# Moving a few dense matmuls around the second attention logits, units 18 to 31

## The chip, the cores and the metric

The kernel runs on one core of one Trainium2 chip. The metric is device time in microseconds (us). TensorE does the matmuls, ScalarE the exponentials and copies, VectorE the elementwise work, GpSimd the masks, and SyncE's queue (SP) the transfers.

## The reference

The input is x, 2048 tokens by 1024. It is layer-normalised to xn, and the output is x + A(xn) + B(xn). B is a token-mixing MLP; it is done before the part at issue. A is attention in four segments of 512 tokens, 32 heads of 32, with a memory carried from segment to segment:

```
q, k, v = x @ wq, x @ wk, x @ wv        # split into heads and 4 segments
for s in range(4):
    p = softmax(qs @ ks.T * scale + causal_mask)
    a_dot = p @ vs
    a_mem = (phi(qs) @ M) / (phi(qs) @ z + 1e-6)   # phi(t) = t+1 if t>0 else exp(t)
    o = g * a_mem + (1 - g) * a_dot
    M, z = M + phi(ks).T @ vs, z + sum(phi(ks))
return o @ wo
```

Matrices are bf16, sums are in float32.

## The kernel before

The first 375 us or so do the norm and the MLP and leave its sum in the output buffer. Then `attention` runs 32 units: unit u is segment u // 8 and a group of four heads, u % 8. An even unit is followed by an odd one, and some of the work is shared by the pair.

The order of the work on every engine is written out by hand. In one unit TensorE does:

- **Logits** of unit u (`logits`, line 1349), in steps. Step 0 holds the first block of keys, step 1 the second and fourth, step 2 (even units only) the third block of this unit and of the next one. Each step fills the four PSUM banks 0 to 3 and is followed by one exponential of 128x2048 on ScalarE (line 1370), which frees these banks, and by masks on GpSimd (line 1374), one per key block. The text calls the steps first, second and third logits.
- **Weighing** of unit u-1 (`weigh`, line 1379), in three parts W0, W1, W2: probabilities times values, and phi(q) times the memory. W0 and W2 use bank 4, W1 bank 5. After each part VectorE copies the result out (ost, line 1424), so W2 waits for the copy of W0. Up to weighing of unit 23, W2 also has four matmuls with pk that update the memory.
- **Dense** matmuls (`dense`, line 1326), which fill the time that the logits and the weighing would wait for other engines. They come from a queue of jobs of eight matmuls of 128x512: value projections (wv), query projections (wq) and output projections of an earlier segment (wo). Jobs alternate between banks 6 and 7. At its eighth matmul a job issues its copy out: ScalarE for wv (vA, line 1299) and wq (qT, line 1253), VectorE for wo (fin, line 1313). A wq job also issues the load of the weights of two units later, on SP.

How many dense matmuls stand in each place is set by `cut`: the unit's total is divided by a tuple of shares, rounded cumulatively. For an even unit the places are: before first logits, before W0, before W1, before W2, before second logits, before third logits, and the rest. An odd unit has no third logits, so its places end with "the rest" after second logits. From unit 18 an even unit has 24 dense matmuls, an odd one 20 and unit 31 has 16.

VectorE's chain for unit u-1 (scales, phi of q, `products`, line 1473, and `add`, line 1479), and then the transpose of its result by SP (oT), are put out one step at a time at stops within the dense jobs (`side`). In even units from 18 on, `products` is done in two halves. `late_exps` puts ScalarE's exponential for phi behind a logits exponential. After unit 31, `tail` does the last output projections.

For units below 18, and for odd units from 18, the shares before the change are:

```
elif u < 10 or u >= 14 and total <= 26:
    cuts = self.cut(total, (0, 4, 2, 4, 1, 13, 8) if even else (7, 3, 2, 4, 1, 15))
```

Of the kernel before, what the change touches and what calls it, by code (L numbers as in the profile page):

```python
# [386 lines left out]
class _Kernel:  # L387
# [1143 lines left out]
    def attention(self):  # L1531
        self.jobs, self.turn, self.left = deque(), 0, 0
        self.side, self.stops = deque(), self.STOPS
        self.exps, self.in_etmp = [], [None] * 4
        self.wo_jobs = deque((c, half) for c in range(4 * (N_SEG - 1)) for half in range(2))
        self.jobs.extend([self.q_job(0), self.k_job(0)] + [self.v_job(0, c) for c in range(4)])
        self.dense(16)
        self.late_exps()
        self.phi_k(0)
        self.k_transpose(0)  # L1540
        self.jobs.extend([self.q_job(1), self.k_job(1)])
        self.dense(100)
        for u in range(N_UNIT):
            if u == N_GRP:
                t, R = _Walk(self.mem, self.B_AT + self.STG_AT, self.B_AT + self.S2_AT).take(
                    "oT2", [P, N_GRP, SEG_L], BF16, N_GRP)
                self.oT.append(t)
                self.R_oT.append(R)
                self.load_fin(0)
                self.load_fin(1)  # L1550
            if 1 <= u <= N_GRP:
                self.fw.dma(self.wo[:, u - 1, :], self.A_wo[(u - 1) * P:u * P, :], writes=[self.R_wo[u - 1]])
            even = u % 2 == 0
            self.jobs.extend(self.unit_jobs(u))
            total = 8 * len(self.jobs) - sum(j[0] for j in self.jobs) - self.left
            xn = self.XN_AT.index(u) + 4 if u in self.XN_AT else None
            if u in self.XN_AT[::4]:
                self.xn_load(xn)
                self.xn_load(xn + 1)
            if u >= 18 and even:  # L1560
                cuts = self.cut(total, (0, 5, 1, 4, 0, 9, 5))
            elif u < 10 or u >= 14 and total <= 26:
                cuts = self.cut(total, (0, 4, 2, 4, 1, 13, 8) if even else (7, 3, 2, 4, 1, 15))
            else:
                cuts = self.cut(total, (0, 4, 2, 2, 2, 14, 8) if even else (7, 3, 2, 2, 2, 16))
            end = u >= N_UNIT - 4
            self.stops = self.STOPS_FEW if total <= 26 and u >= 14 else self.STOPS
            self.dense(cuts[0])
            self.logits(u, 0)
            self.dense(cuts[1], end)  # L1570
            while end and self.side:
                self.side.popleft()()
            if u:
                self.weigh(u - 1, 0)
            self.dense(cuts[2], False)
            if u:
                self.weigh(u - 1, 1)
            self.dense(cuts[3], False)
            if u:
                self.weigh(u - 1, 2)  # L1580
                steps = self.combine(u - 1)
                last = steps[-1]
                steps[-1] = lambda u=u, last=last: (last(), self.o_transpose_dma(u - 1))
                self.side.append(steps.pop(0))
            if N_GRP <= u:
                self.side.append(lambda u=u: self.phi_q(u))
            if u:
                self.side.extend(steps)
            if u + 1 < N_UNIT:
                self.side.append(lambda u=u: (self.phi_k(u + 1), self.k_transpose(u + 1)))  # L1590
            if xn is not None:
                self.side.append(lambda c=xn: (self.xn_scale(c), self.xn_transpose(c), c % 4 < 2 and self.xn_load(c + 2)))
            self.dense(cuts[4])
            self.logits(u, 1)
            if even:
                self.dense(cuts[5])
                self.logits(u, 2)
            self.dense(8 * len(self.jobs) - sum(j[0] for j in self.jobs) - self.left)
        while self.side:
            self.side.popleft()()  # L1600
        self.tail()
# [84 lines left out]
```

## Time and profile before

| | us |
|---|---|
| median of 4 runs | 651.4 (651.3 to 651.52) |
| the profiled execution | 651.63 |
| its span | 649.9 |
| TensorE busy | 639.6 |
| VectorE busy | 435.0 |
| ScalarE busy | 282.3 |
| GpSimd busy | 152.2 |
| one exponential of 128x2048 (line 1370, mean of 80) | 1.877 |
| one mask (line 1374, median of 128) | 0.635 |

Times within a profile count from the start of its span. Units 18 to 31 begin at 530.96. The first logits of the even units 18, 20, ... 30 start at 530.96, 545.67, 560.68, 575.54, 590.27, 604.59 and 618.85. The granted TensorE clock is full in all slices. Matmuls are pipelined, so a row's end reaches into the next row: what counts is the distance from start to start. A row "x5" merges five instructions. A few matmul records are missing; a row then shows one matmul less than the order has, with an unexplained gap of about one matmul beside it.

### The profile page before, as it was taken

Reading aid. Unit: us, or ns where it says so; the run is one execution under the profiler, and the core shown is the slowest. Engines: PE = TensorE matmul, PEld = TensorE weight load, DVE = VectorE, ACT = ScalarE, POOL = GpSimd, SP = SyncE. Lnnn points to the kernel's source line nnn. Section 1 sums busy time; section 2 is a strip of 40 time slices with the busy share of each in tenths; the row PEclk is TensorE's granted clock in tenths of the full one; section 3 lists DMA queues with packets and bytes.
Section 4 is the critical chain, followed back from the end, with each engine's and each line's share of the span. In section 5 each row is a group of like instructions: output and inputs, shape, how many; then the busy total and the mean of one; then the engine's idle time right before and its main releaser. Section 6 shows DMA issues by size and latency. Waiting matters only on the chain.

```text
span 649.9 us, 11137 instructions
## 1 busy us (share of the span) xinstructions
PE 639.6 (98%) x4559; PEld 303.6 (47%) x4611; DVE 435.0 (67%) x813; ACT 282.3 (43%) x307; POOL 152.2 (23%) x179
## 2 busy tenths in 40 slices
PE   8999999999999999999999999999999999999998
PEld 3444444444444444444444444444455454445544
DVE  6975676665556664744637326766887888787896
ACT  7543222232210000110101037778777878889770
POOL 2500000000001220220202203343334444454440
PEclk9999999999999999999999999999999999999999
DMA  8804233233498937538272957989863666445334
GB/s 300 219 0 131 66 104 91 65 113 83 122 261 199 244 113 210 147 112 227 72 219 84 265 126 184 185 177 209 140 143 93 161 163 126 122 104 129 102 96 139
DMA packets 190123, 95.00 MB, mean 146 GB/s; under 512 B 108664, under 2 KB 176248, under 8 KB 190072
## 3 DMA queue, kind: packets, MB, share of 16 engines
q1 hardware_dynamic: 189928, 94.25, 57.3%
q8 instruction: 36, 0.59, 0.4%
q14 instruction: 15, 0.12, 0.1%
q10 hardware_dynamic: 144, 0.03, 0.0%
HBM read 69.23 MB, written 11.53 MB: 124 GB/s over the span
## 4 chain that ended last, share of the span: by engine, by line
PE 93%; DVE 2%; ACT 2%; DMA 2%; issue 1%; POOL 0%; DVEq 0%
PE ps_all L199 93%; ACT pT L1370 1%; DMA w2s<-in_B_w_dram 1%; DVE ln_st L587 1%; DVE sum L648 0%; DMA xin<-in_A_x_dram 0%; DVE h L627 0%; POOL ln_rs L611 0%; DVE part L689 0%; ACT qT L1253 0%; ACT vA L1299 0%; DVE gT L663 0%; DVE ln_mv L590 0%; DVE ln_mv L609 0%; DVE fin L1632 0%
## 5 line engine op out<-in xcount | busy, mean ns | idle before, releaser
L1370 ACT ACTIVATE pT<-ps_all 128x2048 bf16<-128x2048 f32 x80 | 150.2, 1877 | 43.4 <-PE ps_all L199 42.8
L1374 POOL TENSOR_SCALAR_AFFINE_SELECT pT<-pT 128x512 bf16<-128x512 bf16 x128 | 103.7, 828 | 161.7 <-ACT pT L1370 161.7
L689 DVE TENSOR_TENSOR part<-ps_all,part 128x512 f32<-128x512 f32 x84 | 57.7, 690 | 108.9 <-PE ps_all L199 87.9
L1075 POOL TENSOR_TENSOR part<-part,stg 128x512 f32<-128x512 f32 x24 | 33.0, 1402 | 285.4 <-DVE part L689 268.5
L746 ACT ACTIVATE g<-part,b1c 128x512 f16<-128x512 f32 x36 | 26.0, 722 | 99.0 <-DVE part L689 99.0
L199 PE MATMUL ps_all<-wv,xnT 128*128 128x512 bf16 x240 | 64.6, 380 | 1.3 <-ACT qT L1253 0.2
L199 PE MATMUL ps_all<-wo,oT 128*128 128x512 bf16 (+2 forms) x258 | 61.0, 366 | 1.4 <-issue 0.5
L199 PE MATMUL ps_all<-xnT,wq 128*128 128x512 bf16 x240 | 61.3, 380 | 0.5 <-issue 0.3
L694 ACT ACTIVATE part<-ps_all 128x512 f32<-128x512 f32 x24 | 14.0, 596 | 101.7 <-PE ps_all L199 67.1
L199 PEld LDWEIGHTS ps_all<-vA,pT 128*128 128x128 bf16 x1280 | 45.9, 96 | 19.3 <-DVE ost L1424 1.2
L1424 DVE TENSOR_TENSOR ost<-ps_all,eps 128x396 bf16<-128x396 f32 (+1 forms) x72 | 36.9, 520 | 26.2 <-PE ps_all L199 25.7
L199 PE MATMUL ps_all<-g,sum 128*128 128x512 f16 x224 | 51.0, 379 | 0.0
L199 PE MATMUL ps_all<-g,w2s 128*128 128x512 f16 x224 | 51.0, 379 | 0.0
L199 PE MATMUL ps_all<-gT,sum 128*128 128x512 f16 x224 | 50.3, 379 | 0.1
L199 PE MATMUL ps_all<-vA,pT 128*128 128x33 bf16 x1280 | 48.5, 177 | 0.0
L199 PE MATMUL ps_all<-h,sum 128*128 128x512 f16 x192 | 45.2, 379 | 0.0
L199 PE MATMUL ps_all<-h,w1s 128*128 128x512 f16 x192 | 44.9, 379 | 0.0
L199 PE MATMUL ps_all<-hT,sum 128*128 128x512 f16 x192 | 43.6, 379 | 0.0
L1473 DVE TENSOR_TENSOR prod<-ost,srec 128x1024 bf16<-128x1024 bf16 (+1 forms) x31 | 35.9, 1158 | 0.3
L199 PEld LDWEIGHTS ps_all<-wo,oT 128*128 128x128 bf16 x272 | 23.9, 97 | 24.4 <-issue 3.7
L199 PEld LDWEIGHTS ps_all<-xnT,wq 128*128 128x128 bf16 x256 | 22.6, 97 | 25.4 <-issue 5.3
L199 PEld LDWEIGHTS ps_all<-gT,sum 128*128 128x128 f16 x224 | 21.8, 98 | 26.8 <-DVE gT L663 0.6
(119 smaller groups left out, 861.8 us busy)
## 6 DMA issues: line engine op xcount, KB each, us to landing
w2s<-in_B_w_dram SPq DMA_DIRECT2D x8, 1792.0 KB, 9.8
w1s<-in_B_w_dram SPq DMA_DIRECT2D x12, 1024.0 KB, 5.6
wq<-in_A_wq_dram SPq DMA_DIRECT2D x32, 256.0 KB, 3.4
xs<-in_A_x_dram SPq DMA_DIRECT2D x24, 256.0 KB, 3.4
stg<-in_A_x_dram SPq DMA_DIRECT2D x16, 256.0 KB, 2.9
out_dram<-stg SPq DMA_DIRECT2D x16, 256.0 KB, 4.3
wk<-in_A_wk_dram SPq DMA_DIRECT2D x16, 256.0 KB, 3.6
fin<-out_dram SPq DMA_DIRECT2D x16, 256.0 KB, 3.3
```

What stands on the lines that cost most here:

```text
L199: ins = self.nc.tensor.matmul(*args, **kwargs)
L587: fw.op("dve", lambda e: e.bn_stats(st[:, 6 * h:6 * h + 6], src[:, 512 * h:512 * h + 512]), reads=[self.R_xin[c]], writes=[R])
L689: self.fw.op("dve", lambda e: e.tensor_tensor(self.tmp[dst][:], self.bank(b), self.tmp[src][:], op=ALU.add), reads=[self.R_bank[b], self.R ...
L694: self.fw.op("act", lambda e: e.activation(self.tmp[dst][:], self.bank(b), ACT.Copy), reads=[self.R_bank[b]], writes=[self.R_tmp[dst]])
L746: self.fw.op("act", lambda e: e.activation(self.gB[f % 2][half][:, f // 2, :], src, ACT.Gelu_apprx_tanh, bias=self.b1c[:, f:f + 1], scale= ...
L1075: fw.op("pool", lambda e: e.tensor_tensor(self.tmp[t][:], self.tmp[t][:], self.stg[k][:, 512 * half:512 * half + 512], op=ALU.add), reads= ...
L1370: fw.op("act", lambda e: e.activation(dst, src, ACT.Exp, scale=SCALE), reads=self.R_bank[0:4], writes=[R[v % 2][kb] for v, kb, _ in blocks ...
L1374: fw.op("pool", lambda e: e.affine_select(d, d, pattern=[[0, 4], [1, P]], compare_op=ALU.is_ge, fill=0.0, base=0, channel_multiplier=-1), ...
L1424: fw.op("dve", lambda e: e.tensor_tensor(dst, src, eps, op=ALU.add), reads=[self.R_bank[b], self.R_eps], writes=[self.R_ost[o][part]])
L1473: fw.op("dve", lambda e: e.tensor_tensor(self.prod[:, a0:a1], ost[:, a0:a1, 0:D_HEAD], rec[:, a0:a1].unsqueeze(2).to_broadcast([P, a1 - a0 ...
```

## The change

Only shares are changed. Even units from 18 get one share fewer in front of W2 and one more between second and third logits. Odd units from 18 get shares of their own. The jobs, their order and the number of instructions on every engine stay.

```diff
             if u >= 18 and even:
-                cuts = self.cut(total, (0, 5, 1, 4, 0, 9, 5))
+                cuts = self.cut(total, (0, 5, 1, 3, 0, 10, 5))
+            elif u >= 18:
+                cuts = self.cut(total, (4, 1, 2, 1, 0, 12))
             elif u < 10 or u >= 14 and total <= 26:
                 cuts = self.cut(total, (0, 4, 2, 4, 1, 13, 8) if even else (7, 3, 2, 4, 1, 15))
```

## The prediction

> **What bounds the kernel now.** I read the page first: busy rows, the chain that ended last.
>
> ```profile
> PE 639.6 (98%) x4559; PEld 303.6 (47%) x4611; DVE 435.0 (67%) x813; ACT 282.3 (43%) x307; POOL 152.2 (23%) x179
> PE 93%; DVE 2%; ACT 2%; DMA 2%; issue 1%; POOL 0%; DVEq 0%
> ```
>
> TensorE sets the end. A new order of the same matmuls can only win or lose TensorE's idle moments, so I looked for those in units 18 to 31 (530.96 us to the end), first in TensorE's timeline, then in those of its weight loads, ScalarE, VectorE and GpSimd.
>
> ```profile
> 542.66 0.39 PE L199 MATMUL ps_all<-vA,pk 128*128 128x132 bf16 x4
> 543.20 0.40 PE L199 MATMUL ps_all<-qT,kT 32*128 32x384 bf16 x8
> 543.53 1.25 PE L199 MATMUL ps_all<-xnT,wq 128*128 128x512 bf16 x5
> 544.62 1.03 PE L199 MATMUL ps_all<-wo,oT 128*128 128x512 bf16 x4
> 545.67 0.40 PE L199 MATMUL ps_all<-qT,kT 32*128 32x512 bf16 x4
> ```
>
> Unit 19, from the end of its third weighing part (W2) to unit 20's first logits. The prices are here: five dense matmuls from 543.53 to 544.62 are 0.217 us each; a logits group takes 0.33. The four wo matmuls should end at 545.49. A dense-to-logits turn costs 0.10 where nothing is waited for (536.66 plus three matmuls to 537.41), so unit 20's logits should start at 545.58. They start 0.09 later.
>
> ```profile
> 543.65 1.88 ACT L1370 ACTIVATE pT<-ps_all 128x2048 bf16<-128x2048 f32 x1 [1.04 <-PE ps_all L199]
> 545.42 0.59 ACT L1253 ACTIVATE qT<-ps_all 128x512 bf16<-128x512 f32 x1
> 546.11 1.88 ACT L1370 ACTIVATE pT<-ps_all 128x2048 bf16<-128x2048 f32 x1
> ```
>
> ScalarE's exponential of the second logits ends at 545.53; the next logits need the same four banks. Started 0.45 after its logits, it ends 2.33 after them, and nine dense matmuls don't quite cover that.
>
> ```profile
> 545.64 0.13 PEld L199 LDWEIGHTS ps_all<-qT,kT 32*128 32x128 bf16 x4 [0.49 <-issue]
> 549.00 0.47 PEld L199 LDWEIGHTS ps_all<-vA,pT 128*128 128x128 bf16 x16 [0.39 <-DVE ost L1424]
> 561.14 0.77 PEld L199 LDWEIGHTS ps_all<-wv,xnT 128*128 128x128 bf16 x5 [0.36 <-issue]
> ```
>
> Weight loads show three kinds of stop: this one; W2 of unit 20, which waits for VectorE to empty its bank; and unit 22's first dense matmuls, whose bank ScalarE's late vA copy holds until 561.03.
>
> ```profile
> 544.77 0.69 DVE L1230 SCALAR_TENSOR_TENSOR pqT<-qT,mtmp 128x512 bf16<-128x512 bf16 x1
> 545.38 1.72 DVE L1473 TENSOR_TENSOR prod<-ost,srec 128x512 bf16<-128x512 bf16 x2
> 547.80 0.68 DVE L1313 TENSOR_TENSOR fin<-ps_all,fin 128x512 bf16<-128x512 f32 x1
> 548.40 1.03 DVE L1424 TENSOR_TENSOR ost<-ps_all,eps 128x396 bf16<-128x396 f32 x2
> 537.42 1.04 POOL L1374 TENSOR_SCALAR_AFFINE_SELECT pT<-pT 128x512 bf16<-128x512 bf16 x1 [3.29 <-ACT pT L1370]
> 537.88 1.66 DVE L1473 TENSOR_TENSOR prod<-ost,srec 128x1024 bf16<-128x1024 bf16 x1
> 552.20 1.72 POOL L1374 TENSOR_SCALAR_AFFINE_SELECT pT<-pT 128x512 bf16<-128x512 bf16 x1 [3.51 <-ACT pT L1370]
> 552.21 1.22 DVE L1473 TENSOR_TENSOR prod<-ost,srec 128x1024 bf16<-128x1024 bf16 x1
> ```
>
> VectorE runs without a break from unit 19's W2 to unit 20's ost copies. The last four lines are two meetings of VectorE's product with GpSimd's masking: whoever comes second is held.
>
> **The change part by part.** It adds and removes no instruction; it moves dense matmuls within a unit. The cuts (rounded shares) give more than its words say: with 20 matmuls an odd unit goes from 4, 2, 2, 2, 1, 9 to 4, 1, 2, 1, 0, 12. Second logits come three dense matmuls sooner, W2 two, W0 and W1 one. Even units go from 0, 5, 1, 4, 0, 9, 5 to 0, 5, 1, 3, 0, 10, 5: W2 and second logits one sooner, third logits unmoved. Unit 31 (16 matmuls) goes from 4, 1, 1, 2, 0, 8 to 3, 1, 2, 0, 0, 10: its first logits come one sooner, too.
>
> *Gain 1, first logits of units 20, 22, 24, 26, 28, 30.* All start 2.46 or 2.47 after the second logits before them (545.67, 560.68, 575.54, 590.27, 604.59, 618.85), where 2.38 is the work between. Twelve matmuls in place of nine cover ScalarE with 0.56 to spare: 6 x 0.09 = 0.54.
>
> *Gain 2, banks held by a copy behind that exponential.* Unit 22 stands 0.17 (561.01 to 561.18), units 26 and 30 0.07 each. The exponential, 0.65 earlier, lets the copy through in time: 0.31. Two like stops, 0.25 in unit 21 and 0.16 in unit 25, come after an even unit's third logits; their qT copy is behind third logits' exponential, which doesn't move, so they stay.
>
> *Gain 3, W2 of units 20 and 24.* They wait 0.06 each. In even units W2 arrives 0.217 sooner, at 548.64 in unit 20 (with 0.09 from gain 1). Its bank is free 0.61 after the first ost copy starts. VectorE's unbroken chain starts from unit 19's W2, 0.43 sooner: copy at 547.97, bank free at 548.58. The wait goes: 0.12. What covers the even unit's part is thus the odd unit's; without it this edit costs 0.217 a unit. Elsewhere the bank is free in time: in unit 18, where no chain moves, 533.89 against W2's arrival at 534.01.
>
> *Loss, unit 31.* Only eight matmuls are left between unit 30's third logits and unit 31's first: 0.217 of waiting for the exponential. Then 0.33 + 3 x 0.217 + weighing 1.24 + 0.10 = 2.32 lies before second logits, which can't start before 2.38: 0.06. Together 0.27, and all dense work after it is TensorE's own.
>
> *At nothing.* Odd second logits wait for first logits' exponential, 2.38 later at the earliest; the work between is 2.77 (with the four pk matmuls) or 2.54 (from unit 25), so 0.16 to spare. Odd W2 needs its bank 0.79 after W0's end and has 1.07. Masking comes earlier with its exponential. On SP, in units 19, 23 and 27 the q-weight load falls behind the oT transpose: from 544.81 to about 548.7, landing 3.4 later, needed near 558.8; transposes go 0.4 earlier and key loads stay. In unit 31 a fin sum moves behind an ost copy and holds VectorE's chain about 0.5; unit 30's transpose moves from 636.31 to about 636.8, lands 2.4 later and is needed at 639.9. If those covers fail, the tail waits by the excess. Other engines' order is unchanged.
>
> *A rule against the change.* The product 537.88 took 1.66 beside a mask begun first; 552.21, which won, took 1.22: the loss is 0.44. The Trainium skill (SBUF — State Buffer, section "SBUF: two separate sides") says that VectorE's two-input operations and GpSimd share one port pair: "The shared pair is an **exclusive lock**", held for a whole instruction. In unit 19 the product leads the mask by 0.21. The chain moves 0.43, the mask 0.65: a dead heat in units 19, 21, 23. From unit 25 the product led by 0.61 and keeps the lead. By the rule a lost heat costs a whole mask, 0.63 (its usual time); by the row 0.44. Then unit 20's ost copy starts at 548.41, W2 leaves at 549.02 as before, gains 1 and 3 are lost there (0.15), and the matmul moved behind it is added, 0.217: 0.37 each in units 20 and 24, so the sum is +0.04 by the row, +0.42 by the rule. Unit 22 has no fin sum in the way and stands. I take the heat as won: in 552.20 against 552.21 the mask was recorded 0.01 earlier and lost.
>
> Sum: -0.54 - 0.31 - 0.12 + 0.27 = -0.70 us. The profiled execution took 651.63 (span 649.9), 0.23 over the median of 651.4; taken to the median, 650.7.
>
> **Rivals.**
> - *Heat lost*: GpSimd holds VectorE; no net change, 651.4 (651.8 by the rule). For it: the waiting mask won at 537.42. Against: it came 0.46 before the product there.
> - *Less than the sum*: part of the 0.09 is not ScalarE. For it: the trace puts 545.64 down to "issue". Against: unit 18, reached with an older exponential, shows none. Only gains 2, 3 and the loss: 651.2.
> - *More*: unit 21's and 25's stops go with the earlier copies, another 0.41: 650.3.
> - *Slower*: W2 of every even unit stands for its bank, since VectorE does not come forward. All seven moved matmuls are then lost, 7 x 0.217 = 1.52, gains before that point are absorbed, and the 0.27 stays: +1.79, 653.2. It decides where the first ost copy ends later than W2 arrives. Units 28 and 30 would be 0.04 short (606.99 + 0.61 against 607.56) if the chain did not gain its 0.43; units 18, 22 and 26 have 0.12 to 0.3 to spare even then, which speaks against it.
> - *The words aren't the change*: three matmuls instead of two, and unit 31, are counted above; with odd units at two the cover in gain 1 would still be ample.
>
> **How the numbers follow.** My sum 0.47, heat lost 0.23, less 0.12, more 0.10, slower 0.08. The range 650.0 to 652.0 leaves out the slower rival and the edges of the rest. A measurement of this kernel can tell about 0.2%, 1.3 us, from no change: faster means under 650.1, slower over 652.7. All forecasts but "slower" lie inside. Faster 0.10 (most of "more", if it is underrated by 0.2, and a little of my sum), within 0.82, slower 0.08. For the likeliest case alone: 650.3 to 651.0.
>
> **What would show it.** Right: first logits of units 20 to 30 start 0.10 after the last dense matmul; unit 22's dense matmuls follow its logits in 0.33; W2 in units 20 and 24 shows no VectorE wait; a new stop near 0.2 before unit 31's first logits. Wrong: products of 2.1 us in units 19, 21 and 23, weight loads of even W2 waiting for ost, or a wait before jc 6 of the tail's products. A span shorter by over 1.3 or longer at all disproves my sum.

## The result, and the profile after

The changed kernel takes 650.77 us (median of 34 runs), the kernel before 651.51 (52 runs). The ratio is 0.9989, 95% interval 0.9984 to 0.9993: 0.74 us or 0.1% less, and the interval leaves out 1. The profiled execution took 650.8, its span is 649.0.

The busy row of the page after:

```profile
PE 639.5 (99%) x4559; PEld 304.2 (47%) x4611; DVE 435.5 (67%) x813; ACT 282.7 (44%) x307; POOL 153.3 (24%) x179
```

TensorE works as long as before (639.5 against 639.6), in a shorter span. The page cannot say where the idle time went. The starts of the first logits do. Counted from unit 18's first logits of the same trace (530.96 before, 530.83 after: the 0.13 arose in code that the change does not touch), in us; the ends of the spans are taken from the traces to 0.01 (649.89 and 649.03):

| | before | after | difference | summed from the prediction's steps |
|---|---|---|---|---|
| unit 20 | 14.71 | 14.62 | -0.09 | -0.09 |
| unit 22 | 29.72 | 29.47 | -0.25 | -0.24 |
| unit 24 | 44.58 | 44.08 | -0.50 | -0.50 |
| unit 26 | 59.31 | 58.63 | -0.68 | -0.65 |
| unit 28 | 73.63 | 72.79 | -0.84 | -0.81 |
| unit 30 | 87.89 | 86.95 | -0.94 | -0.90 |
| unit 31 | 96.56 | 95.55 | -1.01 | -0.97 |
| end of the span | 118.93 | 118.20 | -0.73 | -0.70 |

TensorE's timeline after, from unit 19's W2 to unit 20's first logits:

```profile
542.10 0.39 PE L199 MATMUL ps_all<-vA,pk 128*128 128x132 bf16 x4
542.42 0.40 PE L199 MATMUL ps_all<-qT,kT 32*128 32x384 bf16 x8
542.98 1.67 PE L199 MATMUL ps_all<-xnT,wq 128*128 128x512 bf16 x7 [0.16 <-issue]
544.49 1.03 PE L199 MATMUL ps_all<-wo,oT 128*128 128x512 bf16 x4
545.45 0.39 PE L199 MATMUL ps_all<-qT,kT 32*128 32x512 bf16 x4
```

Second logits follow W2 at once, and twelve dense matmuls follow them (eight wq, of which one record is missing in front of 542.98, and four wo). The wo matmuls should end at 544.49 + 4 x 0.217 = 545.36, and unit 20's logits start at 545.45: only the turn's 0.09 to 0.10 is left.

ScalarE in the same place:

```profile
542.87 1.88 ACT L1370 ACTIVATE pT<-ps_all 128x2048 bf16<-128x2048 f32 x1 [0.40 <-PE ps_all L199]
545.90 1.88 ACT L1370 ACTIVATE pT<-ps_all 128x2048 bf16<-128x2048 f32 x1 [0.61 <-PE ps_all L199]
```

Second logits' exponential ends at 544.75, 0.70 ahead of the logits that need its banks. Before, these were 0.14 apart; and now it is ScalarE that waits 0.61 for TensorE.

Unit 22's dense matmuls, which had to wait for their bank before, now follow its logits (560.30 + 0.33):

```profile
560.62 0.76 PEld L199 LDWEIGHTS ps_all<-wv,xnT 128*128 128x128 bf16 x5 [0.23 <-issue]
```

Every block begins with some idle time of the weight loads: 0.20 to 0.23 in front of dense matmuls, 0.42 to 0.43 at a turn to logits. The loads of units 18 to 31 that stand longer are these, and unit 24's W2, which reads as unit 20's:

```profile
548.45 0.52 PEld L199 LDWEIGHTS ps_all<-vA,pT 128*128 128x128 bf16 x16 [0.27 <-DVE ost L1424]
554.82 0.10 PEld L199 LDWEIGHTS ps_all<-wv,xnT 128*128 128x128 bf16 x1 [0.45 <-issue]
584.22 0.10 PEld L199 LDWEIGHTS ps_all<-wv,xnT 128*128 128x128 bf16 x1 [0.39 <-ACT qT L1253]
626.37 0.10 PEld L199 LDWEIGHTS ps_all<-qT,kT 32*128 32x128 bf16 x4 [0.64 <-ACT pT L1370]
```

The first is W2 of unit 20: the load is released by VectorE, but the matmul follows when the dense ones end (547.87 + 3 x 0.217 = 548.52, started 548.51), so the 0.27 costs nothing. The next two are the stops of units 21 and 25 behind the qT copy, which stayed. The last is new: unit 31's first logits, with a matmul less in front of them.

VectorE and GpSimd at the place of the dead heat:

```profile
544.82 1.72 DVE L1473 TENSOR_TENSOR prod<-ost,srec 128x512 bf16<-128x512 bf16 x2
546.58 0.74 DVE L1479 TENSOR_TENSOR o_s<-prod 128x512 bf16<-128x512 bf16 x1
547.84 1.03 DVE L1424 TENSOR_TENSOR ost<-ps_all,eps 128x396 bf16<-128x396 f32 x2
544.82 2.22 POOL L1374 TENSOR_SCALAR_AFFINE_SELECT pT<-pT 128x512 bf16<-128x512 bf16 x2 [2.13 <-ACT pT L1370]
```

Product and mask start at the same hundredth, and the product wins: 1.72 as before, and the two masks take 2.22 instead of 2.01. The row of the product is two instructions, one for each half. The first half takes 0.68; the second, while the first mask runs, takes 1.00, before as after. So to win here means that the first half is not held.

In the tail a product of the same kind lost. Unit 30's product and add, and the masks of unit 31, after; then product and add before:

```profile
631.75 2.15 DVE L1473 TENSOR_TENSOR prod<-ost,srec 128x512 bf16<-128x512 bf16 x2
634.43 0.41 DVE L1479 TENSOR_TENSOR o_s<-prod 128x512 bf16<-128x512 bf16 x1
631.15 2.21 POOL L1374 TENSOR_SCALAR_AFFINE_SELECT pT<-pT 128x512 bf16<-128x512 bf16 x2 [1.75 <-ACT pT L1370]
632.23 1.72 DVE L1473 TENSOR_TENSOR prod<-ost,srec 128x512 bf16<-128x512 bf16 x2
634.48 0.41 DVE L1479 TENSOR_TENSOR o_s<-prod 128x512 bf16<-128x512 bf16 x1
```

Here the mask came 0.60 ahead of the product (0.21 behind it before), and product and add, with a fin sum between them, are 2.68 apart instead of 2.25: the whole 0.43 stays in the chain. TensorE did not wait for it: SyncE's queue was busy with a load until 635.34, 0.50 after the add's end, and took up the transpose then, earlier than before (635.39, before 636.31).

### The profile page after: what moved, and what is told of

Same layout as the page of the kernel before. It is cut to its first block, busy times and chain, and to the rows that moved or that the text cites. A ratio compares the mean times of both kernels' runs of the same rounds, so it can differ in the third digit from the quotient of the medians.

```text
span 649.0 us, 11134 instructions
## 1 busy us (share of the span) xinstructions
PE 639.5 (99%) x4559; PEld 304.2 (47%) x4611; DVE 435.5 (67%) x813; ACT 282.7 (44%) x307; POOL 153.3 (24%) x179
## 4 chain that ended last, share of the span: by engine, by line
PE 96%; ACT 1%; DVE 1%; issue 1%; DMA 0%; POOL 0%; DVEq 0%
PE ps_all L199 96%; ACT pT L1370 1%; DVE ln_st L587 1%; DMA xin<-in_A_x_dram 0%; DVE h L627 0%; POOL ln_rs L611 0%; ACT qT L1253 0%; DVE ln_mv L590 0%; DVE ln_mv L609 0%; DVE fin L1634 0%; PE ps_all L205 0%; DVEq L70 0%
```

## The experiments

The kernel before stood at 651.39 in the session of the first four kernels and at 651.40 in that of the last three. The last column, unit 18's first logits to the end of the span, leaves out the differences between profiles ahead of the change; the kernel before has 118.93 there, the changed one 118.20. The diffs are against the changed kernel, and the last one against the version that it names; "..." stands for lines left out.

| kernel | median, us | ratio to before, 95% | unit 18 to end |
|---|---|---|---|
| e1_odd_only | 650.70 | 0.9989 (0.998 to 0.9997) | 118.21 |
| e2_even_only | 651.82 | 1.0006 (0.9997 to 1.0015) | 119.34 |
| e3_not_unit31 | 650.35 | 0.9983 (0.9975 to 0.9992) | 117.92 |
| e4_odd_one_sooner | 650.82 | 0.9991 (0.9982 to 1.0) | 118.31 |
| e5_heat_lost | 651.50 | 1.0002 (0.9993 to 1.001) | 119.02 |
| e6_delay_no_heat | 651.09 | 0.9995 (0.9987 to 1.0004) | 118.51 |
| e8_w0_first | 650.01 | 0.9979 (0.997 to 0.9988) | 117.51 |

The intervals are as wide as the effects, some 1.1 us, and those of e2, e4, e5 and e6 take in no change. What follows rests on the places in the traces, one profile of each kernel, more than on the medians.

**Odd part alone.** The even line keeps its old shares:

```diff
-                cuts = self.cut(total, (0, 5, 1, 3, 0, 10, 5))
+                cuts = self.cut(total, (0, 5, 1, 4, 0, 9, 5))
```

> Only the odd units' new shares; even units as before. My theory: the odd part carries all of the gain (first logits of units 20 to 30 no longer wait for ScalarE, W2 of units 20 and 24 no longer waits for VectorE), and the even part only moves a matmul inside covered time. So the time is that of the whole change, 0.7 us under before, and W2 of unit 20 shows no VectorE wait with 0.2 us to spare. Rival: the even part carries a share of its own (second logits sooner, ScalarE sooner); then only 0.3 to 0.5 us under before.

Measured: 0.69 under before, 0.72 in the trace; the whole change has 0.74 and 0.73. The odd part carries the gain; the even part adds 0.05 at most, which these runs do not tell from nothing. Weight loads of unit 20's W2 in this kernel, a row without any releaser:

```profile
548.36 0.67 PEld L199 LDWEIGHTS ps_all<-vA,pT 128*128 128x128 bf16 x16
```

**Even part alone.** The new odd line is taken out:

```diff
-            elif u >= 18:
-                cuts = self.cut(total, (4, 1, 2, 1, 0, 12))
```

> Only the even units' new shares; odd units as before. My theory: VectorE's chain does not come forward, so W2 of units 20 and 24 arrives 0.22 sooner and waits 0.28 instead of 0.06, the moved matmul is added behind it: 0.22 each, 0.44 us slower than before, 651.9; the 0.09 waits before first logits of units 20 to 30 stay. Rival: harmless alone, within 0.1 of before. Second rival (the slower one of the prediction): W2 stands in all seven even units, 1.5 us slower.

Measured: 0.43 slower than before, 0.41 in the trace. Its weight loads:

```profile
545.35 0.13 PEld L199 LDWEIGHTS ps_all<-qT,kT 32*128 32x128 bf16 x4 [0.49 <-issue]
548.73 0.47 PEld L199 LDWEIGHTS ps_all<-vA,pT 128*128 128x128 bf16 x16 [0.61 <-DVE ost L1424]
607.74 0.52 PEld L199 LDWEIGHTS ps_all<-vA,pT 128*128 128x128 bf16 x16 [0.27 <-DVE ost L1424]
```

The idle time in front of W2 in units 20 and 24 (578.82) grew from 0.39 to 0.61, by the one matmul that went behind it. The row with 0.27 (unit 28) costs nothing: unit 30's first logits start 14.25 after unit 28's, and 14.26 before. The wait behind "issue" is still there in front of unit 20's first logits. So the even part alone costs a matmul in two units and nothing in five, and is a loss, as my theory had it; the prediction's slower rival, all seven units, is refuted.

**Unit 31 as before, the rest changed.**

```diff
-            elif u >= 18:
+            elif 18 <= u < N_UNIT - 1:
                 cuts = self.cut(total, (4, 1, 2, 1, 0, 12))
```

> Both parts, but unit 31 keeps its old shares (4, 1, 1, 2, 0, 8). My theory: the 0.22 wait before unit 31's first logits goes and its second logits no longer wait, so 0.27 us better than the whole change: 0.97 under before, about 650.5. Rival: TensorE catches up in the tail anyway (the tail has waits of its own), same as the whole change.

Measured: 1.04 under before, 1.01 in the trace, 0.28 better than the whole change there. TensorE's timeline, third logits of unit 30 and first logits of unit 31:

```profile
623.87 0.40 PE L199 MATMUL ps_all<-qT,kT 32*128 32x256 bf16 x8
624.20 2.12 PE L199 MATMUL ps_all<-wo,oT 128*128 128x512 bf16 x9
626.25 0.40 PE L199 MATMUL ps_all<-qT,kT 32*128 32x512 bf16 x4
```

The logits are 2.38 apart, and 2.39 in the changed kernel (623.99 to 626.38), but with nine matmuls between them and no wait. What unit 31 loses is not made good in the tail.

**Odd units with one matmul moved.** W0, W1 and W2 stay; only the matmul that stood in front of second logits goes behind them. Even units and unit 31 are as before:

```diff
-                cuts = self.cut(total, (0, 5, 1, 3, 0, 10, 5))
-            elif u >= 18:
-                cuts = self.cut(total, (4, 1, 2, 1, 0, 12))
+                cuts = self.cut(total, (0, 5, 1, 4, 0, 9, 5))
+            elif 18 <= u < N_UNIT - 1:
+                cuts = self.cut(total, (4, 2, 2, 2, 0, 10))
```

> Odd units from 18 to 29 get (4, 2, 2, 2, 0, 10): only the last dense matmul in front of second logits moves behind them, W0, W1 and W2 stay; even units and unit 31 as before. My theory: one matmul (0.22) is enough for the 0.09 wait, but VectorE's chain stays, so in units 20 and 24 W2 still leaves when the bank is free and the 0.09 is lost there: gain 4 x 0.09 + 0.12 + 0.14 = 0.62 us under before, with a W2 wait of about 0.15 in units 20 and 24. Rival: VectorE doesn't matter, only ScalarE does: 0.85 under before and no W2 wait.

Measured: 0.57 under before, 0.62 in the trace. The weight loads of unit 20's W2:

```profile
548.82 0.47 PEld L199 LDWEIGHTS ps_all<-vA,pT 128*128 128x128 bf16 x16 [0.49 <-DVE ost L1424]
```

All "issue" waits in front of first logits are gone: a single matmul is enough for them. But the idle time in front of this W2 is 0.49, 0.10 more than before: TensorE comes 0.09 sooner to a bank that VectorE frees when it did. Both coverings are needed, ScalarE's exponential earlier and VectorE's chain earlier, and it is the earlier W2 of the odd unit that gives the second one.

**The heat lost.** "Heat" is the tie of product and mask. In the changed kernel a small VectorE operation of odd units, the min for phi, is done twice ahead of the product (the second gives the same values again):

```diff
             k = u % 3
+            if u >= 19 and u % 2:
+                self.again(u)
             self.phi(self.pqT[k][:], self.R_pqT[k], self.qT[k][:], self.R_qT[k], 0, u)
...
+    def again(self, u):
+        n = 2 * (u % 2)
+        self.fw.op("dve", lambda e: e.tensor_scalar(self.mtmp[0][:], self.etmp[n][:], 1.0, None, op0=ALU.min),
+                   reads=[self.R_etmp[n]], writes=[self.R_mtmp[0]])
```

> The whole change, and in odd units from 19 VectorE's small min operation for phi (0.28 to 0.31 us, same operands, same result) is done twice, ahead of the product: the product comes 0.31 later, GpSimd's mask does not. My theory: the mask, asked for while pqT still runs, wins the ports, the products of units 19, 21 and 23 take about 2.15 instead of 1.72; VectorE's chain is 0.31 + 0.43 later, W2 of units 20 and 24 waits about 0.7, units 22, 28 and 30 a little (0.1 to 0.3): 1.4 to 2.0 us slower than the whole change. Rival: a lost heat costs nothing (the order of product and mask does not matter to TensorE), then 0.5 slower, as its sister below.

Its sister does the same operation, by the same `again`, after the product:

```diff
-                steps[-1] = lambda u=u, last=last: (last(), self.o_transpose_dma(u - 1))
+                steps[-1] = lambda u=u, last=last: (u >= 19 and u % 2 and self.again(u), last(), self.o_transpose_dma(u - 1))
```

> The same second min operation, but behind the product and ahead of the final add: VectorE's chain is 0.31 later with the heat untouched. My theory: products stay at 1.72; W2 of units 20 and 24 waits 0.27 each, the other even units have room: 0.54 us slower than the whole change, 651.3. Rival: W2 has spare time beyond what I read (first ost copy to bank free is less than 0.61): no change against the whole change.

Measured, against the changed kernel (118.20 from unit 18 to the end): 0.82 slower with the heat lost, 0.31 slower with the delay alone. VectorE and GpSimd in unit 19, heat lost:

```profile
544.61 0.69 DVE L1230 SCALAR_TENSOR_TENSOR pqT<-qT,mtmp 128x512 bf16<-128x512 bf16 x1
545.22 2.15 DVE L1480 TENSOR_TENSOR prod<-ost,srec 128x512 bf16<-128x512 bf16 x2
547.41 0.42 DVE L1486 TENSOR_TENSOR o_s<-prod 128x512 bf16<-128x512 bf16 x1
544.88 1.95 POOL L1381 TENSOR_SCALAR_AFFINE_SELECT pT<-pT 128x512 bf16<-128x512 bf16 x2 [2.14 <-ACT pT L1377]
```

The delay alone, where the product keeps its 1.72:

```profile
546.23 0.72 DVE L1240 TENSOR_SCALAR mtmp<-etmp 128x512 bf16<-128x512 bf16 x1
546.87 0.41 DVE L1484 TENSOR_TENSOR o_s<-prod 128x512 bf16<-128x512 bf16 x1
```

The mechanism is as expected: with the mask 0.34 ahead of the product, the product takes 2.15 (units 21 and 23: 2.16). Both sizes were missed. I had expected 1.4 to 2.0 and 0.54. With the heat won, the second mask is still waiting when the product ends, and the final add is held for it (0.74); with the heat lost, masks are done by then and the add takes 0.42. The 0.43 lost in the product comes back, but for about 0.11. In the sister it is the added operation that meets the mask (0.72 instead of 0.29) and the add that is spared, so that it costs about 0.2 of the chain and not 0.32. W2 had 0.06 to spare, so in two units 0.32 + 0.11 makes some 0.74, and 0.2 some 0.28. The order of product and mask moves one wait between three operations more than it adds one, as long as the add follows the product directly; in the tail, where it does not, 0.43 stayed.

**W0 straight behind first logits.** On top of the version with unit 31 as before:

```diff
-                cuts = self.cut(total, (4, 1, 2, 1, 0, 12))
+                cuts = self.cut(total, (4, 0, 3, 1, 0, 12))
```

> As the version with unit 31's old shares, and odd units get (4, 0, 3, 1, 0, 12): W0 straight behind first logits, the dense matmul that stood there goes between W0 and W1. In units 21 and 25 that matmul's bank is held by the qT copy behind third logits' exponential for 0.25 and 0.16; W0 (0.36) now fills this time. My theory: both stops go, 0.41 us better than the version with unit 31's old shares: 1.38 under before, about 650.0, faster than every version so far. Rival: W0, one matmul earlier, waits for VectorE or a mask in its turn (VectorE's fin sum ends just in time in unit 19): same as that version, or slower.

Measured: 1.39 under before, 1.42 in the trace, 0.41 better there than the version it is built on. Unit 21 in TensorE's timeline (two more rows of W0, from 554.81 to 555.07, left out):

```profile
554.37 0.40 PE L199 MATMUL ps_all<-qT,kT 32*128 32x512 bf16 x4
554.69 0.27 PE L199 MATMUL ps_all<-vA,pT 128*128 128x33 bf16 x4
555.07 0.81 PE L199 MATMUL ps_all<-wv,xnT 128*128 128x512 bf16 x3
```

W0 fills the time until the qT copy frees the wv matmuls' bank. At 650.01 this is the fastest of the kernels that were run.

## Why the prediction was right, point by point

- *Gain 1*, 6 x 0.09: shown. First logits of units 20 to 30 follow the dense matmuls at the turn's price; one moved matmul suffices for it, and with the odd units as before the wait stays. The turn's price had been read in a row (537.41) that starts 2.38 after the logits ahead of it, which is ScalarE's limit as well; the trace after has the same 0.09 to 0.10 with the exponential 0.70 ahead, so it is the turn's.
- *Gain 2*, banks held by a copy: shown in place for unit 22, where 0.17 of the step from 0.25 to 0.50 in the table is this. Unit 21's and 25's stops stayed, as predicted, which rules out the rival "more"; the last experiment shows their size, 0.41.
- *Gain 3*, W2 of units 20 and 24: shown, and with it that the odd part covers the even one. But "without it this edit costs 0.217 a unit" was too wide: alone it costs that in units 20 and 24, and nothing in the other five. Units 28 and 30, which the slower rival reckons 0.04 short when VectorE's chain does not come forward, lost nothing there.
- *Unit 31*: predicted 0.27 lost, 0.28 in the table (from -1.01 to -0.73), 0.28 by undoing it.
- *At nothing*: the q-weight load of unit 19 went behind the transpose, from 544.81 to 548.59, and nothing waited for it. In the tail unit 30's transpose was even issued earlier (635.39, where 636.8 was feared), since the load in front of it took 0.43 to issue instead of 1.30. Why it did is open, so this was luck, and it hid two terms that were wrong. VectorE's chain stood 1.05 for unit 31's fin sum (629.24 to 630.33, less a usual gap of 0.04), where about 0.5 was reckoned; and unit 30's product lost its meeting with the mask, which the prediction did not look for in the tail.
- *The rule and the heat*: the product won, in a tie to 0.01; the prediction had one earlier row to go by. The price of a lost heat was the term that was mis-sized. The row's 0.44 is right for the product, but the rival took it as a delay of the whole chain; in unit 19 it is about 0.11. Had the heat been lost, unit 20 would have been later by an estimated 0.05, not by 0.37: 0.11 less the 0.06 that W2 had to spare (bank free at 547.84 + 0.61 = 548.45, W2 at 548.51). By this estimate the sum hardly hung on who won. The rule's whole mask, 0.63, was not seen: 0.43 was.
- *"Issue"*: the rival "less than the sum" doubted that 0.09 is ScalarE's. It disappears with an earlier exponential in every version with second logits sooner. Why TensorE starts 0.11 after the exponential's end in that row, and GpSimd's mask 0.06 after it, was not tested.

## What to carry to other kernels

When one engine is the bound and almost always busy, look for its idle time between starts, 0.1 us at a time, and name for each piece what had to be done first; then sum only over the places where the new order makes that earlier. A moved piece of cover has to be paid for where it came from: here the even units' matmul was free only because the odd units' change had brought VectorE forward, and the last unit, cut by the same shares with fewer matmuls, paid a quarter of the gain back. Use a cut per place, not a share for all.

## What the runs showed of the hardware that was not expected

Two operations of VectorE and GpSimd that meet do not simply add a wait. With the product first, its halves took 0.68 and 1.00 and the add, beside the second mask, 0.74: with the gaps, 1.72 + 0.74 = 2.46. With the mask first they took 1.12, 1.00 and 0.42: 2.15 + 0.42 = 2.57. Two of the three operations are held in either order. In the tail the add was 0.41 in either order, and the lost meeting cost its whole 0.43. And a tie to a hundredth (544.82 for both in unit 19; 559.68 against 559.67 and 574.29 against 574.28 in units 21 and 23) went to VectorE's operation each time, with products of 1.72, while a mask that came 0.34 earlier (0.60 in the tail), during VectorE's operation before, got in between.
